# Interleaving early attention with projections and scan inputs, and feeding the late attention with single scan operations and single matmuls

## The chip, the cores and the metric

The kernel runs on one core of one Trainium2 chip. The metric is the device time of that core in microseconds (us), as the median of several executions. A profiled execution also gives a *span*, from its first to its last instruction, which is 1.9 us shorter than the time of the same execution here (180.44 and 178.5 us before). Each execution is marked fast or slow: slow means more than 1.5% above the fastest of the same kernel. Comparisons below use fast executions unless the text says otherwise.

The engines are PE (matmul), PEld (its weight loads, which overlap PE), DVE (vector), ACT (scalar), POOL and SP. SP does nothing here but issue DMAs.

## The reference

Two independent layers read two inputs of 2048 rows by 448 columns. Their outputs stand side by side in the result.

```python
def _A_ref(x, wqkv, wo):                  # local attention, 16 heads of 28
    q, k, v = split_heads(x @ wqkv)
    # row s sees rows s, s-2, ..., s-14 (8 of them, dilation 2)
    attn = softmax(where(mask, q . k[idx] * scale, -1e9))
    return merge_heads(attn . v[idx]) @ wo

def _B_ref(x, ...):                       # complex diagonal state space layer
    Bu = x @ B_bar.T
    for t in range(2048):
        h = Lam_bar * h + Bu[t]           # 448 complex states
    return 2 * real(hs @ Cmat.T) + x * Dskip

return concatenate([a, b], axis=-1)       # 2048 x 896, bfloat16
```

## The kernel before

Even and odd rows are handled apart, so that layer B scans over 1024 pairs of rows and the dilated window of layer A becomes a dense one. Its work comes in these pieces:

- `proj_qk` and `proj_v` (tiles `pq`, `pv`): the projections of layer A.
- `bu(s, pt)` (tile `pb`): scan inputs, for two halves `s` of time and four groups `pt` of states. `scan(s, hf)` is a scan on DVE over two groups.
- `step(n)`: scores (`sp`) of attention block n on PE, the exponential (`P`) on ACT, and the product with the values (`op`) of block n-1. There are 18 blocks.
- Normalization of the attention in three stages, after blocks 7, 13 and 17: the row sums are written to DRAM and read back spread over partitions (`dc`), inverted (`rf`), written to DRAM, read back as a broadcast (`rd`), and multiplied into the attention output (`qT`, the same storage as `oT`).
- `y_tile(n)` (tile `py`): 18 matmuls give 256 output rows of layer B; ACT and DVE each evacuate a half (`yb`). `wo_tile(n)` (tile `pw`): 8 matmuls give 256 output rows of layer A (`ya`).

All of `pq`, `pv`, `pb`, `sp`, `py` and `pw` share three PSUM buffers, called `ps2`. Each engine executes its instructions in the order of the program text once `hold` is set.

```python
def norm_load(k):
    ...                                                # [cut]
    nc.sync.dma_start(s1[:], oT[DH:128:32, :, :, c0:c0 + w_])
    dc = at.tile([128, QB], BF16, tag="dc", name="dc")
    nc.sync.dma_start(dc[0:r_, :], s1[:]...)           # [cut]
    rf = at.tile([128, QB], F32, tag="rf", name="rf")
    V.reciprocal(rf[0:r_], dc[0:r_])
    rb = at.tile([128, QB], BF16, tag="rb", name="rb")
    V.tensor_copy(rb[0:r_], rf[0:r_])
    ...                                                # [cut: a check; s2 <- rb; four broadcasts rd <- s2]

def norm(k):
    V.tensor_tensor(o_, o_, att["rd", k][:]..., ALU.mult)

def scan(s, hf):                                       # 12 to 16 DVE operations in a row
    ...
    V.tensor_tensor(c_, z, sinb, ALU.mult)
    V.tensor_tensor(z, z, cosb, ALU.mult)
    V.tensor_tensor(z[:, 0], z[:, 0], c_[:, 1], ALU.add)
    V.tensor_tensor(z[:, 1], z[:, 1], c_[:, 0], ALU.subtract)
    for ri in range(2):
        for i in range(2):
            V.tensor_tensor_scan(c_[:, ri, i, :], ...)
    ...                                                # [cut: carry if s == 0; then 4 more]

def y_tile(n):
    ps = ps2.tile([128, 2, 512], F32, tag="s", name="py")
    ...                                                # [cut: 11 matmuls into half 0, 7 into half 1]
    ACT.copy(yb[:, 0, :], ps[:, 0, 0:D])
    V.tensor_tensor(yb[:, 1, :], ps[:, 1, 0:D], xD[:, n, :], ALU.add)
    nc.sync.dma_start(out_b[n, :, :, D:2 * D], yb[:])

# after the start: projections of the second half, woven only with small weight products
weave([L(proj_qk, qk, par, 1, gp) for gp, par, qk in QK] + [L(proj_v, b) for b in range(4, NB)], fl)
bz_open()
hold[0] = True

def step(n):
    if n < NA:
        att_s(n)
    if 0 < n <= NA:
        att_pv(n - 1)
        if n in (8, 14, 18):
            norm_load((8, 14, 18).index(n))

for s_ in range(2):
    for pt in range(4):
        bu(s_, pt)
        if pt % 2:
            scan(s_, pt // 2)
        step(4 * s_ + pt)
k0_make(0)
step(8)
k0_make(1)
step(9)
step(10)
for k in range(4):
    if k % 2:
        norm(k // 2)
    y_tile(k)
    step(11 + 2 * k)
    step(12 + 2 * k)
for n in range(3):
    wo_tile(n, "A")
y_tile(4)
for n in range(3, 6):
    wo_tile(n)
y_tile(5)
norm(2)
...                                                    # [cut: y 6, wo 6 and 7, a check, y 7]
```

The loads of `wo` and of `xD` (the odd rows of B's input, for the skip term) are issued from the POOL queue at the start of the program.

## Time and profile before

| | before |
|---|---|
| time, median of 3 | 179.55 us (179.32 to 180.45) |
| span of the profiled execution | 178.5 us |
| PE busy | 141.3 us, 79% |
| DVE busy, ACT busy | 110.3 us, 98.4 us |
| longest idle time of PE | 12.47 us |
| scores of block 8 start | 95.94 us |
| last matmul ends, end of span | 171.3, 178.5 us |

These lines are from the page of the profile of the kernel before: busy shares in tenths in 40 slices of 4.46 us each (9 is 90% or more); PEclk is the granted PE clock in tenths.

```profile
PE   7673896999999989899999891009787969999930
...
DVE  2308999988698108999999999980224040624410
...
PEclk9979699999999999999999998555969999999996
```

From slice 9 to 24 PE is at 8 or 9. In slices 25 to 27 (107 to 120 us) it shows 1, 0, 0, where DVE shows 9, 9, 8, and the clock falls to 5. What happened there is in the timeline of the kernel before. Its columns are the start, the duration, engine and line, operation, output and inputs with shapes, count, and in brackets the idle time before it and what ended it. The full list has ACT and weight loads between these lines.

```profile
105.63 1.22 DVE L135 TENSOR_TENSOR sc<-Z,tab 128x2048 bf16<-128x2048 bf16 x1
...
106.71 0.37 PE L135 MATMUL sp<-mB,mA 32*128 32x456 bf16 x4
...
109.48 4.81 DVE L135 TENSOR_TENSOR_SCAN sc<-rT,ini,Z 128x512 bf16<-128x512 f32 x4
...
116.84 1.29 DVE L135 TENSOR_TENSOR Hs<-Hs,sc 128x1024 bf16<-128x1024 bf16 x2
118.05 0.86 DVE L135 RECIPROCAL rf<-dc 128x114 f32<-128x114 bf16 x1
...
119.40 0.62 DVE L135 TENSOR_TENSOR yb<-py,xD 128x448 bf16<-128x448 f32 x1
120.07 0.57 PE L135 MATMUL sp<-mB,mA 32*128 32x456 bf16 x4 [12.47 <-DVE yb L135]
...
121.46 1.68 PE L135 MATMUL py<-K_178,xTB 128*128 128x448 bf16 x4
```

From 105.63 to 118.05 us DVE works through the last scan, 12.4 us. The reciprocal of the first normalization and its small operations come next, and only at 119.40 us the addition `yb`, which reads the PSUM buffer of y tile 0. PE could issue scores at 106.71 us; for the next ones it needed the buffer of `ps2` that `yb` reads, and waited 12.47 us. The next matmuls of y take 0.42 us each (1.68 us for 4), where those of y tile 0 took 0.21 (1.49 us for 7, not shown): half clock. The Trainium skill ("TensorE: Matmul & The Clock Gate", Part 1) says that an idle window of about 3.4 us lets the clock fall to half, and this agrees.

The list of what PE waited for, in total, times and longest, puts that wait first.

```profile
engine line waited for: us in total, times, longest us
PE sp L135 <- DVE yb L135: 12.5, 1, 12.5
PE sp L135 <- ACT P L135: 2.9, 5, 0.8
```

Busy time of each engine by stretches of the kernel before shows the losses around it (in parentheses the count of instructions):

```profile
core 0: us, PE busy (x) PEld busy (x) DVE busy (x) ACT busy (x) POOL busy (x), PEclk, DMA share, GB/s
...
110.00:120.00 10.00, 0.00 (x0) 0.00 (x0) 9.83 (x13) 0.00 (x0) 0.00 (x0) 0.53 0.00 0
...
130.00:146.00 16.00, 13.05 (x165) 6.56 (x165) 3.90 (x8) 9.76 (x15) 0.00 (x0) 0.89 0.29 78
```

In the gap PE does nothing at all and DVE is busy 9.83 of 10 us. From 130 to 146 us PE is busy 13.05 of 16 us, with pauses for ACT's `P`, which is 1.75 us for each block.

### The profile page before, as it was taken

To read this page: it belongs to the slowest core of one execution; us is meant where nothing else is said; L and a number is where in the kernel's file an instruction comes from. 1 tells how busy PE (TensorE), PEld (TensorE's weight loads), DVE (VectorE), ACT (ScalarE), POOL (GpSimd) and SP (SyncE) were. 2 spreads that over 40 slices of the span, in tenths; PEclk is the share of its full clock that TensorE was granted. 3 is DMA by queue.
4 is the path that set the end of the run, shared out by engine and by line. 5 is a ranking of instruction groups with operands and counts; after the bars stand their busy time and mean duration, and the time that the engine had idled before them with its cause. 6 is when DMAs were issued, how large, how long until landed. Compare 5 with 4: busy or idle time off the path is not lost. (4 is left out here: it accounts for less than half of the span.)

```text
span 178.5 us, 3078 instructions
## 1 busy us (share of the span) xinstructions
PE 141.3 (79%) x1217; PEld 68.6 (38%) x1227; DVE 110.3 (62%) x194; ACT 98.4 (55%) x142; POOL 13.0 (7%) x31
## 2 busy tenths in 40 slices
PE   7673896999999989899999891009787969999930
PEld 2231342444445444444445440004433535555410
DVE  2308999988698108999999999980224040624410
ACT  2006899699886297777777765004645573322210
POOL 8990000000000000000000000000000000000000
PEclk9979699999999999999999998555969999999996
DMA  5999999999900000000000000006411704273320
GB/s 109 202 271 258 285 191 218 184 186 177 210 0 4 0 0 0 4 0 4 0 4 0 13 4 0 0 7 167 99 36 34 190 21 143 76 252 110 105 84 30
DMA packets 34262, 16.40 MB, mean 92 GB/s; under 512 B 27376, under 2 KB 33460, under 8 KB 34244
## 3 DMA queue, kind: packets, MB, share of 16 engines
q1 hardware_dynamic: 33676, 14.55, 35.6%
q0 software_dynamic: 560, 1.61, 3.4%
q8 instruction: 11, 0.18, 0.4%
q14 instruction: 7, 0.06, 0.1%
q10 hardware_dynamic: 8, 0.00, 0.0%
HBM read 5.90 MB, written 3.80 MB: 54 GB/s over the span
## 5 line engine op out<-in xcount | busy, mean ns | idle before, releaser
L135 ACT ACTIVATE P<-sp 128x912 bf16<-128x912 f32 x36 | 31.6, 934 | 12.2 <-PE sp L135 12.1
L137 PE MATMUL pq<-xTA,wqk 128*128 128x512 bf16 x125 | 28.2, 381 | 2.2 <-DVE kT L137 1.7
L135 PE MATMUL pb<-xTB,BT 128*128 128x512 bf16 x105 | 25.1, 379 | 2.6 <-ACT Z L135 2.3
L137 PE MATMUL pv<-wv,xTA 128*128 128x448 bf16 x72 | 17.0, 399 | 4.3 <-ACT vp L137 2.5
L135 PE MATMUL sp<-mB,mA 32*128 32x456 bf16 x72 | 8.0, 371 | 15.6 <-DVE yb L135 12.5
L137 PEld LDWEIGHTS <-wqk 128*128 128x128 bf16 x128 | 12.7, 99 | 17.7 <-issue 3.4
L135 PEld LDWEIGHTS <-BT 128*128 128x128 bf16 x112 | 10.9, 97 | 14.3 <-issue 2.1
L135 ACT CAST yb<-py 128x448 bf16<-128x448 f32 x8 | 4.3, 532 | 22.0 <-PE py L135 22.0
L135 PEld LDWEIGHTS <-Hs 128*128 128x128 bf16 x112 | 11.7, 105 | 12.1 <-issue 3.2
L135 DVE TENSOR_TENSOR qT<-qT,rd 128x3648 bf16<-128x3648 bf16 (+2 forms) x3 | 4.7, 1580 | 15.6 <-DMA rd<-s_1259 8.1
L135 PE MATMUL py<-WL,Hs 128*128 128x448 bf16 x56 | 13.9, 395 | 0.0
L135 ACT CAST Z<-pb 128x1024 bf16<-128x1024 f32 x8 | 8.1, 1012 | 9.4 <-PE pb L135 9.4
L137 PEld LDWEIGHTS <-xTA 128*128 128x128 bf16 x72 | 7.7, 108 | 12.8 <-issue 7.9
L135 PE MATMUL pw<-wo,qT 128*128 128x448 bf16 x64 | 12.6, 353 | 0.0
L135 PE MATMUL py<-Wt,Hs 128*128 128x448 bf16 x56 | 12.2, 359 | 0.0
L135 PEld LDWEIGHTS <-mA 32*128 32x128 bf16 x72 | 2.4, 91 | 21.9 <-issue 21.4
L135 DVE TENSOR_TENSOR sc<-Z,tab 128x2048 bf16<-128x2048 bf16 x4 | 4.9, 1226 | 9.2 <-ACT Z L135 8.9
L135 ACT CAST qT<-op 128x456 bf16<-128x456 f32 x18 | 10.0, 554 | 0.0
L137 DVE CAST kT<-pq 128x1024 bf16<-128x1024 f32 x8 | 9.8, 1222 | 0.2 <-PE pq L137 0.2
L135 DVE TENSOR_TENSOR_SCAN sc<-rT,ini,Z 128x512 bf16<-128x512 f32 x8 | 9.6, 1265 | 0.1
L135 DVE TENSOR_TENSOR yb<-py,xD 128x448 bf16<-128x448 f32 x8 | 5.0, 620 | 7.1 <-ACT yb L135 7.1
L135 DVE RECIPROCAL rf<-dc 128x114 f32<-128x114 bf16 (+2 forms) x3 | 2.6, 859 | 10.9 <-DMA dc<-s_1800 6.4
(142 smaller groups left out, 207.8 us busy)
## 6 DMA issues: line engine op xcount, KB each, us to landing
out_dram<-yb SPq DMA_DIRECT2D x8, 224.0 KB
out_dram<-ya SPq DMA_DIRECT2D x8, 224.0 KB, 2.7
rd<-s_1259 SPq DMA_DIRECT2D x4, 228.0 KB, 5.0
xD<-in_B_x_dram POOLq DMA_DIRECT2D x1, 896.0 KB, 9.2
rd<-s_1599 SPq DMA_DIRECT2D x4, 171.0 KB, 2.7
wraw<-in_A_wqkv_dram SPq DMA_DIRECT2D x3, 224.0 KB
rd<-s_1809 SPq DMA_DIRECT2D x4, 114.0 KB, 2.6
wo<-in_A_wo_dram POOLq DMA_DIRECT2D x4, 98.0 KB, 3.9
```

The source lines that it names most:

```text
L135: r = f(*a, **k)
L137: r = f(*a, **k)
```

## The change

The intent is to take DVE's last scan off the way of PE and to give PE something to do in each pause. It has five parts:

1. *Weave.* `pb` tiles, the second-half projections and attention blocks 0 to 7 are put in one hand-made order, so that scans start early and ACT's exponentials are spread over a longer time. `hold` is set only after the weave; before that the order on an engine need not be that of the text.
2. *Cut scan.* The last scan becomes 12 single DVE operations; two of them follow each attention step.
3. *Nines.* y and wo products become lists of single matmuls, and nine of them are issued after each attention step.
4. *Split reciprocals.* `norm_inv` (the inverse, and the way back through DRAM) is split from `norm_load`, and comes some steps later.
5. *Late loads.* `xD` is loaded near the end of the weave (issued at 84.59 us in the trace) and `wo` after it (99.26 us) rather than at the start, into space that is free by then. The scans also work in place in `Hs`.

The diff holds smaller edits outside these five: `P` gets three buffers instead of two, some loads and transposes at the start come in another order, the scheduler may choose the engine that evacuates the second-half projections, and DVE instead of ACT copies wo tiles 0 to 2.

```diff
@@ norm_load @@
         nc.sync.dma_start(dc[0:r_, :], s1[:]...)          # [shortened]
-        rf = at.tile([128, QB], F32, tag="rf", name="rf")
+        att["dc", k] = dc
+
+    def norm_inv(k):
+        dc = att["dc", k]
+        rf = zz["at"].tile([128, QB], F32, tag="rf", name="rf")
         V.reciprocal(rf[0:r_], dc[0:r_])
@@ y_tile, in the same way wo_tile @@
-    def y_tile(n):
+    def y_parts(n):
+        t = {}
+        def mm(i, lhs, rhs, start, stop):
+            if not t:
+                t["ps"] = ps2.tile([128, 2, 512], F32, tag="s", name="py")
+            PE.matmul(t["ps"][:, i, 0:D], lhs, rhs, start=start, stop=stop)
+            if i and stop:
+                ...                                        # [cut: evacuation and store]
+        return [L(mm, 0, xTB[:, kt, xs], K0[:, kt, :], kt == 0, False) for kt in range(4)] + ...
@@ scan: the same operations as a list, scan_parts(s, hf) [cut] @@
@@ late loads @@
-    for j in range(4):
-        POOL.dma_start(wo[32 * j:32 * j + DH, :, :], wo_r[j])
-    POOL.dma_start(xD[:, 0:n_, :], B_x[0]...[1])
+    def late_open():
+        pj_ctx.close()
+        ...                                                # [cut: wo loaded here]
+    def xd_load():
+        xD = zz["xD"] = st.tile([128, n_ + 1, D], BF16, tag="NB", name="xD")
+        POOL.dma_start(xD[:, 0:n_, :], B_x[0]...[1])
@@ main part @@
-    weave([L(proj_qk, ...)] + [L(proj_v, b) for b in range(4, NB)], fl)
-    bz_open()
-    hold[0] = True
-    for s_ in range(2):
-        for pt in range(4):
-            bu(s_, pt)
-            if pt % 2:
-                scan(s_, pt // 2)
-            step(4 * s_ + pt)
-    ...
+    for x in "pbwpbwpsbwpspwbsplblpsblplskbpkpsbpkspsp":
+        {"p": PJ, "b": BU, "s": ST, "w": WM, "l": WLM, "k": KM}[x].pop(0)()
+    for s_, hf in ((0, 0), (0, 1), (1, 0)):
+        scan(s_, hf)
+    late_open()
+    hold[0] = True
+    fill = []
+    dq = scan_parts(1, 1)
+
+    def spend(k, d=0):
+        while k > 0 and fill:
+            fill.pop(0)()
+            k -= 1
+        for _ in range(d):
+            if dq:
+                dq.pop(0)()
+
+    skip_make()
+    for n in range(4):
+        fill += y_parts(n)
+    for n in range(8, NA + 1):
+        step(n)
+        if n == 11:
+            norm_inv(0)
+        if n == 14:
+            norm(0)
+            for k in range(3):
+                fill += wo_parts(k, "D")
+            fill += y_parts(4)
+        if n == 17:
+            norm_inv(1)
+        spend(9, 2)
+    spend(10)
+    norm(1)
+    for k in range(3, 6):
+        fill += wo_parts(k, "D")
+    spend(18)
+    norm_inv(2)
+    spend(1000)
+    for n in (5, 6):
+        fill += y_parts(n)
+    spend(1000)
     norm(2)
     ...                                                    # [cut: wo 6 and 7, check, y 7]
```

## The prediction

> **What bounds the kernel now.** The span is 178.5 us; the busy table gives PE 141.3 (79%), DVE 110.3, ACT 98.4. The table by stretches of 10 us shows three parts. From 28 to 107 us PE is dense (9 to 10 of each 10 us). From 107.5 to 120.07 PE does nothing while DVE is full: the timeline has the whole last scan, then a reciprocal, and only then the `yb` of y tile 0. The list of waits has "PE sp <- DVE yb 12.5 us": the next scores need the PSUM buffer that this `yb` reads. After it matmuls issue every 0.37 us for a while, against 0.19 later. From 120 to 146 us PE also pauses 0.5 to 0.8 us at each pair of attention blocks, waiting for ACT's P (1.76 us a block). There the chain of waits runs through PE; from the last matmul (171.3) to the end are 7.2 us.
>
> From 102.5 to 171.3 us (68.8) PE had 8 y tiles (18 matmuls at 0.187 = 3.36 us each), 8 wo tiles (1.49) and 8 attention steps (about 0.82): 45.4 us of work. So about 23 us are lost.
>
> **What the change does.** It adds and removes almost no work; it moves it. (1) The `pb` tiles, the second-half projections and attention blocks 0 to 7 are woven: first scan at about 49 us, against 67.4. (2) The last scan is cut into 12 pieces, two per attention step, so `yb` waits for about 2.5 us of DVE work instead of 9 or more. (3) y and wo products are issued nine matmuls (1.7 us) after each attention step, just what covers ACT's 1.76. The reciprocals are split from their loads; the xD and wo loads (1.3 MB) move from the crowded start to later.
>
> **Arithmetic, by hand with the trace's durations.** In the weave PE has about 54 us left after the first `pb` (done about 43.5), ACT about 48, with three PSUM buffers. Stepping through it I get the scores of block 8 at about 100.5 us, no better than before (95.9): weaving dense work gains nothing by itself. After that PE has 46.6 us. Added waits:
> - ACT at 2.6 us per step against PE's 2.5: 1.4 us.
> - Second normalization: inverse to broadcast took 8.3 us (136.2 to 144.7), plus 1.6 for the product; PE has about 6 us of filler: 4 us idle.
> - Third: 2 us idle.
> - Cold clock after those: 1.5 us.
>
> PE ends near 156.5; the end of 7.2 us makes a span of 164, and with 1 us between span and time, 165.
>
> **On the critical path:** gained are 12.5 us of idle, some 4 of half clock, 3 to 4 of ACT pauses and a few others; lost are 5 us of later attention and 6 to 8 of normalization waits: about 14.5 net.
>
> The Trainium skill ("TensorE: Matmul & The Clock Gate", Part 1) says an idle window of about 3.4 us drops the clock to half; this trace agrees after the 12.5 us idle (0.37 against 0.19 us). So whether the normalization stalls stay below that matters.
>
> **Predicted time: 165 us, 8 in 10 between 159 and 172.** Faster by over 2%: 0.94; within 2%: 0.04; slower: 0.02.
>
> **Right if the profile shows:** no PE idle over 5 us after 40 us; PE busy above 85%; first scan before 52 us; scores of block 8 at 97 to 104; DVE `yb` no longer the first wait; new waits of DVE `qT` for the DMA `rd`, and PE `pw` waiting for DVE `qT` 2 to 5 us.
>
> **Wrong if:** ACT is overloaded in the weave (block 8 after 106); the xD load, which reuses the NB buffer, lands late and blocks DVE; or the normalization waits exceed 5 us each and let the clock drop.

## The result, and the profile after

| | before | after |
|---|---|---|
| time, median | 179.68 us (179.32 to 180.45, 4 runs) | 163.41 us (163.43, 163.23, 163.38 fast; 167.03 slow) |
| ratio of the fast runs, 95% interval | 1 | 0.9086, 0.9048 to 0.9124 |
| span of the profiled execution, granted clock | 178.5 us, 0.924 | 161.6 us, 0.995 |
| PE busy | 141.3 us, 79% | 135.7 us, 84% |
| first scan starts | 67.44 us | 44.85 us |
| scores of block 8 start | 95.94 us | 97.24 us |
| last matmul ends | 171.3 us | 155.0 us |
| longest idle time of PE after 40 us | 12.47 us | 2.34 us |

A ratio is the mean time of one kernel's fast runs over that of the other's of the same rounds, so it is not quite the ratio of the medians quoted. The output is correct.

The same rows of the page, of the changed kernel (a slice is 4.04 us here):

```profile
PE   7575699989989979999999999898897977994930
...
DVE  3009999995589999999999640399855536815310
...
PEclk9999999999999999999999999999999999999997
```

The gap in PE's row is gone and the clock stays at 9 to the last slice but one. PE has nearly the same instructions; 5.6 us of its busy time are gone where matmuls took longer before: the groups of instructions show 399 and then 352 ns for one `pv` matmul, and 395 and then 353 ns for one of `py` with `WL`.

Where the time came from can be read by stage. From the scores of block 8 to PE's last matmul went 171.3 - 95.94 = 75.4 us before, and 155.0 - 97.24 = 57.8 us after: 17.6 us less. To the scores of block 8 the changed kernel takes 1.3 us *more*, and the end after the last matmul shrank by 0.6 us. Together that is the 16.9 us between the spans. (One of the two `K0` products stood after block 8 before, from 97.07 to 100.12 us, and stands in the weave now. So some 3 us of the 17.6 are work that moved to the stage in front, which in turn began 2.2 us earlier: its first `pq` starts at 18.67 instead of 20.86 us.)

The timeline of the changed kernel around y tile 0, which answers to the one shown of before:

```profile
101.55 1.49 PE L135 MATMUL py<-Wt,Hs 128*128 128x448 bf16 x7
...
103.68 0.62 DVE L135 TENSOR_TENSOR yb<-py,xD 128x448 bf16<-128x448 f32 x1 [8.73 <-ACT yb L135]
...
104.36 0.92 PE L135 MATMUL py<-K_172,xTB 128*128 128x448 bf16 x4 [0.50 <-DVE yb L135]
...
105.54 1.28 DVE L135 TENSOR_TENSOR_SCAN sc<-rT,ini,Hs 128x512 bf16<-128x512 f32 x1
```

Now `yb` of y tile 0 starts 0.64 us after its last matmul ends at 103.04, with pieces of the scan behind it, and PE waits 0.50 us instead of 12.47. The new waits stand in the list of what PE waited for in the changed kernel:

```profile
PE pw L135 <- DVE qT L135: 4.4, 2, 2.3
...
PE py L135 <- DVE yb L135: 1.4, 3, 0.5
```

The first of them are the second and the third normalization. This is the second, in the timeline of the changed kernel; `s_1790` is the DRAM buffer in the middle of the way back:

```profile
125.60 0.31 SPq L395 DMA_DIRECT2D s_1790<-rb  x1
...
127.15 1.70 SPq L398 DMA_DIRECT2D rd<-s_1790  x4
...
130.79 1.49 PE L135 MATMUL py<-Wt,Hs 128*128 128x448 bf16 x7
...
132.66 1.58 DVE L135 TENSOR_TENSOR qT<-qT,rd 128x2736 bf16<-128x2736 bf16 x1 [2.66 <-DMA rd<-s_1790]
...
134.30 3.96 PE L135 MATMUL pw<-wo,qT 128*128 128x448 bf16 x20 [2.03 <-DVE qT L135]
```

The inverse is sent to DRAM at 125.60 us, the four broadcasts are issued from 127.15 us, and the last one lets the multiplication on DVE start at 132.66 us. PE's fill work, here the last 7 matmuls of y tile 4, is used up at 132.28 us, so it waits 2.03 us. The third normalization costs 2.34 us at 148.17 us in the same way.

Busy time by stretches of the changed kernel, with the columns of before; from 121 to 155 us is where PE still idles:

```profile
98.00:121.00 23.00, 21.22 (x372) 11.00 (x364) 14.77 (x18) 19.60 (x29) 3.34 (x5) 1.00 0.38 96
121.00:137.00 16.00, 12.80 (x125) 6.33 (x118) 8.31 (x12) 5.46 (x9) 0.00 (x0) 1.00 0.40 120
137.00:155.00 18.00, 15.63 (x82) 7.61 (x80) 7.43 (x16) 1.97 (x3) 0.00 (x0) 1.00 0.37 118
```

### The profile page after: what moved, and what is told of

The parts are those of the page before. It is cut to its first block, busy times and chain, and to the rows that moved or that the text cites. A ratio compares the mean times of both kernels' runs of the same rounds, so it can differ in the third digit from the quotient of the medians.

```text
span 161.6 us, 3078 instructions
## 1 busy us (share of the span) xinstructions
PE 135.7 (84%) x1218; PEld 65.5 (41%) x1227; DVE 109.2 (68%) x195; ACT 96.9 (60%) x141; POOL 12.8 (8%) x31
## 4 chain that ended last, share of the span: by engine, by line
PE 43%; DVE 22%; ACT 15%; DMA 8%; SPq 5%; issue 3%; DVEq 0%; ACTq 0%
PE py L135 12%; PE pb L137 11%; PE pw L135 6%; PE pq L137 4%; DVE sc L137 4%; PE pk L137 4%; ACT P L135 3%; PE pv L137 3%; DVE Hs L137 3%; DMA rd<-s_1790 3%; SPq L200 2%; ACT P L137 2%; DMA wraw<-in_A_wqkv_dram 2%; DMA BT<-NB__94 2%; DVE NB__94 L137 2%
## 5 line engine op out<-in xcount | busy, mean ns | idle before, releaser
L135 ACT ACTIVATE P<-sp 128x912 bf16<-128x912 f32 x20 | 17.6, 939 | 5.4 <-PE sp L135 5.4
L137 PEld LDWEIGHTS <-wqk 128*128 128x128 bf16 x128 | 12.5, 97 | 18.1 <-issue 3.6
L137 PE MATMUL pv<-wv,xTA 128*128 128x448 bf16 x72 | 14.9, 352 | 5.3 <-POOL K_172 L496 1.9
L135 DVE TENSOR_TENSOR yb<-py,xD 128x448 bf16<-128x448 f32 x8 | 5.0, 624 | 16.9 <-ACT yb L135 16.8
L135 PEld LDWEIGHTS <-Hs 128*128 128x128 bf16 x112 | 10.7, 98 | 9.9
L135 DVE CAST ya<-pw 128x896 bf16<-128x896 f32 x7 | 7.5, 1087 | 7.8 <-PE pw L135 7.8
L135 PE MATMUL py<-WL,Hs 128*128 128x448 bf16 x56 | 12.6, 353 | 0.0
L137 ACT CAST Hs<-pb 128x1024 bf16<-128x1024 f32 x8 | 8.0, 1004 | 7.0 <-PE pb L137 7.0
L135 PEld LDWEIGHTS <-qT 128*128 128x128 bf16 x64 | 5.9, 98 | 11.0 <-DVE qT L135 5.2
L137 DVE TENSOR_TENSOR_SCAN sc<-rT,Hs 128x512 bf16<-128x512 f32 x8 | 9.1, 1204 | 0.1
L135 PE MATMUL py<-K_172,xTB 128*128 128x448 bf16 x32 | 7.4, 352 | 1.8 <-DVE yb L135 1.4
L137 DVE TENSOR_TENSOR Hs<-Hs,sc 128x1024 bf16<-128x1024 bf16 x12 | 7.8, 687 | 0.2
L137 ACT COPY wqk<-wraw 128x896 bf16<-128x896 bf16 (+1 forms) x2 | 1.9, 936 | 9.0 <-DMA wraw<-in_A_wqkv_dram 8.9
```

The costliest lines, as they stand in the source:

```text
L135: r = f(*a, **k)
L137: r = f(*a, **k)
```

## The experiments

All twelve kernels gave correct results. They ran in four batches, each on one chip, with runs of the kernel before beside them (median 180.4 to 180.8 us in each). Only one batch holds the unaltered changed kernel (ref_after), so most variants are compared with it across chips. In the first batch single runs of the kernel before spread from 178.2 to 182.7 us, and its verdicts were recorded as unclear (none for e_inv_at_load, which has one fast run), although the intervals lie well below 0.98; differences of a microsecond between batches should not be read.

The first theory was: the idle time comes from the last scan's position on DVE in front of `yb`, so that cutting it is what counts. The rival was: the early start of the scans (the weave) is what counts.

### a_split_only: the kernel before with only the last scan cut

```diff
+    dq = scan_parts(1, 1)        # the 12 operations of scan(1, 1) as a list
     for s_ in range(2):
         for pt in range(4):
             bu(s_, pt)
-            if pt % 2:
+            if pt % 2 and (s_, pt) != (1, 3):
                 scan(s_, pt // 2)
     ...
         y_tile(k)
+        pieces(2)                # issues the next 2 of dq
         step(11 + 2 * k)
+        pieces(2)
         step(12 + 2 * k)
```

> The kernel before with one thing changed: the last scan is cut into its 12 pieces, two after each y tile or attention step from y tile 0 on; no weave, no nines, loads as before. Theory 1 (the gain comes from taking the undivided last scan out of the way of yb, by whatever means): the 12.5 us idle of PE goes, and most of the half clock after it; but the product of the first normalization now waits on DVE for its broadcast ahead of yb of y tile 1, which may cost PE up to 5 us. 164 to 170 us, PE idle before a scores matmul under 2 us. Rival 1 (the weave, that is the earlier start of the scans, makes the gain, and cutting alone only spreads the same DVE work): 174 us or more.

Measured: 167.55 us in the median (fast runs 166.55 to 167.56), ratio 0.930 (0.921 to 0.938). The profiled execution was slow; in it the wait of 12.5 us is gone:

```profile
108.52 0.62 DVE L135 TENSOR_TENSOR yb<-py,xD 128x448 bf16<-128x448 f32 x1 [0.53 <-ACT yb L135]
...
109.20 0.67 PE L135 MATMUL sp<-mB,mA 32*128 32x456 bf16 x4 [0.45 <-DVE yb L135]
```

The scores that had waited 12.47 us now wait 0.45 us, and the longest wait of scores for ACT's `P` is 0.8 us. The wait of up to 5 us that was feared for y tile 1 did not come (the longest wait of `py` for a `yb` is 0.8 us). One part of the five, by itself, gives three quarters of the gain (1 - 0.930 against 1 - 0.909). The rival, that it needs the weave, falls.

### c_whole_scan: the changed kernel with the last scan whole again

```diff
     skip_make()
+    while dq:
+        dq.pop(0)()
```

> The changed kernel with the last scan issued whole, after the product for xD and before the first yb. Theory 1 in its strict form (the cut is needed): yb 0 waits about 12 us again and the time is 170 us or more. Theory 2 (weave or cut is enough, either one): the scan then runs from about 92.5 to 104.8 us, yb of y tile 0 is wanted at 103.1, so PE loses only 1 to 2 us: 164 to 166 us.

Measured: 166.11 us (165.03 to 167.37), ratio 0.923 (0.914 to 0.932). With scans started early, `yb` of y tile 0 came at 105.31 instead of 103.68 us, and PE's longest wait for a `yb` was 1.9 us. So cutting is worth only 2 to 3 us *in the presence of the weave*. The strict form of the theory, "only the cut counts", falls as well: the early scans, with the rest of the change around them, remove most of the same wait without the cut. (The weave alone, in the kernel before, was not run.)

### g_no_weave: the changed kernel with the old order of the early work

```diff
-    for x in "pbwpbwpsbwpspwbsplblpsblplskbpkpsbpkspsp":
+    for x in "pwpwpwpwplplplplpppppHbsbcsbsbcsbsbcsbsbskkk":   # c: a whole scan, H: hold[0] = True
```

> The changed kernel with the weave undone: all second-half projections and weight preparation first, then pb with attention blocks 0 to 7 and the scans in order, then the products for y; from block 8 on as changed (pieces, nines, split normalization, late loads). If the weave matters because it starts the scans earlier: the first scan starts about 60 us, xD and the pieces about 10 us later than PE needs them, PE waits about 5 us for yb of y tile 0: 167 to 172 us. If the pieces make it unnecessary: 163 to 165 us.

Measured: 168.95 us (fast 167.41, 168.01, 169.90), ratio 0.933 (0.925 to 0.941), against 164.15 us of the unaltered changed kernel in the same batch. The timeline of this kernel shows what the weave had been protecting:

```profile
101.55 2.02 DVE L135 TENSOR_TENSOR xD<-xD 128x3584 bf16<-128x3584 bf16 x1
...
105.88 0.62 DVE L135 TENSOR_TENSOR yb<-py,xD 128x448 bf16<-128x448 f32 x1
...
106.55 1.65 PE L135 MATMUL py<-K,xTB 128*128 128x448 bf16 x4 [5.02 <-DVE yb L135]
```

The third scan ends later, so the skip product (`xD`, 2.02 us) starts at 101.55 us instead of 90.54. It and the first pieces of the last scan (from 103.48 us) stand in front of `yb` of y tile 0, which comes at 105.88 us; PE waits 5.02 us for it, and the next four matmuls run at half clock (1.65 us). Undoing the weave costs about 4.3 us (the difference of the fast means, 168.4 and 164.1 us). In its own stage, though, the weave costs time: without it the scores of block 8 start at 95.09 us instead of 97.24, after the same start (first `pq` at 18.75 and 18.67 us) and the same work. The edit also sets `hold` at its old place, so the freedom to reorder is undone with the weave.

### d_no_nines: whole y tiles after every second step

```diff
-        spend(9, 2)
-    spend(10)
+        spend(18 if n % 2 else 0, 2)
+    spend(19)
```

> The changed kernel with the 18 matmuls of a y tile issued together after every second attention step, instead of nine after each. If the nines cover ACT's 1.76 us per block: about 1.2 us more of pauses per pair of blocks, five pairs, less about 0.5 us per pair saved elsewhere: 3 to 5 us slower, 166.5 to 168.5 us. If they do nothing: 163.4 us.

Measured: 165.06 us (fast 162.79 to 165.13), ratio 0.920 (0.912 to 0.928). In the traces two steps and 18 matmuls take 6.29 us (103.69 to 109.98) instead of 5.82 (100.33 to 106.15), so the nines do cover some of ACT's time. But the profiled execution, 162.79 us, was as short as any of the changed kernel: in it PE waited only once for the normalization, 2.3 us, instead of twice, 4.4 us. Being later at the second normalization, it found it done. What the nines gain is handed back at the next wait, at least in part: 0 to 2 us remain (fast means 164.4 against 163.4 and 164.1 us), and this test does not say which. Neither expectation, 166.5 to 168.5 or 163.4 us, was met.

### e_inv_at_load: each reciprocal directly after its load, as before

```diff
         att["dc", k] = dc
+        norm_inv(k)
...
-        if n == 11:
-            norm_inv(0)
...                               # [cut: the other two calls go too]
```

> The changed kernel with each reciprocal issued straight after the loads of its sums, as in the kernel before. If the separation matters: DVE stands before the reciprocal until dc lands (3 to 5 us each), holding back yb and the scan: 2 to 6 us slower for stages 1 and 2, partly paid back because the broadcasts are there sooner (the two waits of pw for qT, 4.4 us in sum, shrink). Net 164 to 168 us. If it is idle motion: 163.4 us within 0.5.

Measured: 179.54 us in the median; one fast run of 175.07 us and three slow ones of 179.5 to 179.9. No theory expected that much: the fast run is 11.7 us above the changed kernel's fast mean of 163.35 (another batch, on another chip). Its timeline, from a slow execution, shows where the loss begins:

```profile
90.78 2.03 DVE L135 TENSOR_TENSOR xD<-xD 128x3584 bf16<-128x3584 bf16 x1 [1.48 <-PE pb L137]
...
103.64 0.35 SPq L383 DMA_DIRECT2D dc<-s  x1
...
105.48 0.87 DVE L135 RECIPROCAL rf<-dc 128x114 f32<-128x114 bf16 x1 [12.68 <-DMA dc<-s]
...
109.91 0.56 PE L135 MATMUL sp<-mB,mA 32*128 32x456 bf16 x2 [2.87 <-DVE yb L135]
```

The reciprocal stands behind the skip product in DVE's order, but its data `dc` has still to come through DRAM: the load is issued at 103.64 us. DVE waits 12.68 us for it, from 92.8 to 105.48 us, and everything behind it, all pieces of the scan and `yb`, waits too. The Trainium skill ("TensorE: Matmul & The Clock Gate", Part 1, "Architectural detail: the array is 16× 32×32, not 1× 128×128") calls the queues of ACT and DVE strict FIFO; this wait agrees.

The 12.68 us are idle time of DVE, not of PE. PE waits 2.87 us for `yb`, works at half clock for a while, and starts y tile 2 at 116.12 us, where the changed kernel starts it at 110.15. So the first wait makes about 6 us of lag. At the start of y tile 4 the lag is 12.6 us (141.28 against 128.71). What adds to it is a wait of 3.31 us for the normalized `qT` and half clock after it (nine matmuls of `pw` take 3.54 us instead of 1.88). Over the whole trace PE waits 9.6 us for `qT` in three waits, against 4.4 us in two, and is busy 148.0 us with the work that took 135.7. This trace is a slow one, so how the 11.7 us of the fast run divide among the waits and the clock stays open.

In the kernel before, this position did no harm at the first reciprocal: it came behind a scan of 12.4 us, and its data was there (no wait is shown at 118.05 us; the second and third waited 4.5 and 6.4 us, and the list of PE's waits shows none behind them). In a_split_only, too, the first follows the scan before it without a wait; only the third waits, 8.4 us. So the cut alone does not need the split reciprocals. With the scans started early they are needed, here with the cut and in the next run without it, and the prediction gave them no value.

### j_whole_inv_load: both of the last two

```diff
     skip_make()
+    while dq:
+        dq.pop(0)()
...
+        norm_inv(k)              # at the end of norm_load, and not where it was
```

> The changed kernel with the last scan whole and each reciprocal straight after its load: the weave without cutting and without splitting the normalization. If the loss with the reciprocal at its load (175 to 180 us) came from the first reciprocal waiting for dc in front of the scan pieces and yb, the whole scan now fills that wait and the first stage costs under 2 us; what remains is the second reciprocal's 4 us wait and its sequel: 167 to 171 us. If splitting the normalization matters in itself: 175 us or more.

Measured: 173.65 us (173.22 to 174.41), ratio 0.963 (0.957 to 0.968), between the two expectations. The whole scan gave the first reciprocal time, as in the kernel before: it waited 0.20 us. But the second waited 5.55 us and the third 4.68 us, and PE waited 10.4 us in 3 for normalized `qT`. The head-of-queue wait comes back wherever no long DVE work hides it.

### ref_after: the changed kernel again, unaltered

> The changed kernel itself, unaltered, so that the variants have it on the same chip: 163.4 us, 161 to 166.

Measured: 164.15 us (164.87, 163.44, 164.93, 163.30), ratio 0.909 (0.903 to 0.915). This batch's chip repeats the gain. Its profiled execution, 164.87 us, is useful beside the first one, 163.43 us. After the second normalization's wait (2.29 us in this trace, 2.03 us in the other) its 24 matmuls of `pw` read

```profile
134.28 6.40 PE L135 MATMUL pw<-wo,qT 128*128 128x448 bf16 x24 [2.29 <-DVE qT L135]
```

6.40 us, where the other execution shows 4.71 us in the same grouping. A pause of nearly the same length led to half clock here and not there.

### f_tail: the end in another order

The two waits of 2.03 and 2.34 us were the largest left, so the wo tiles that need the second normalization were put behind y tile 5 and the third inverse, and wo tiles 6 and 7 last.

```diff
-    spend(10)
-    norm(1)
-    for k in range(3, 6):
-        fill += wo_parts(k, "D")
-    spend(18)
-    norm_inv(2)
     spend(1000)
-    for n in (5, 6):
-        fill += y_parts(n)
+    norm(1)
+    fill += y_parts(5)
     spend(1000)
-    norm(2)
+    norm_inv(2)
     ...                          # [cut: the check]
-    fill += wo_parts(6) + wo_parts(7)
+    for k in range(3, 6):
+        fill += wo_parts(k, "D")
+    fill += y_parts(6)
     ...                          # [cut: the check's end, y 7]
+    norm(2)
+    fill += wo_parts(6) + wo_parts(7)
```

> The changed kernel with its end in another order: y tile 4 is finished and y tile 5 is made before wo tiles 3 to 5, y tiles 6 and 7 are made before wo tiles 6 and 7, and the check of the sums moves ahead of y tile 7. The two waits of pw for the product qT (2.0 and 2.3 us) should go; no work is added. 4 us faster than the changed kernel: 159 us. If the waits only move to another place (the third broadcast then lands later than the work lasts), less than 2 us faster.

Measured: 165.41 us (165.02 to 166.22), ratio 0.917 (0.911 to 0.922): 1.4 us slower than the changed kernel of the same batch, a miss. From the timeline of this kernel:

```profile
138.02 0.56 SPq L383 DMA_DIRECT2D dc<-s  x1
...
140.16 0.86 DVE L135 RECIPROCAL rf<-dc 64x114 f32<-64x114 bf16 x1 [2.81 <-DMA dc<-s]
...
143.24 1.65 PE L135 MATMUL py<-K,xTB 128*128 128x448 bf16 x4 [2.57 <-DVE ya L135]
```

The load of `dc` stood in the SP queue behind a store that itself waited for `yb` of y tile 5, and was issued at 138.02 us. The third reciprocal waited 2.81 us for it on DVE, in front of the `ya` copies, and PE waited 2.57 us for a `ya`; four matmuls then took 1.65 us, half clock. The wait had been moved, not removed, in the same manner as in e_inv_at_load.

### h_tail_no_nines: f_tail without nines

```diff
-        spend(9, 2)
+        spend(18 if n % 2 else 0, 2)
```

> The kernel with the reordered end, but y tiles issued whole after every second attention step. In the changed kernel the nines took 5.8 us per pair of steps against 6.3 without them, and the time was the same. Theory: the nines gain 2 to 2.5 us in the attention stage and the wait for the second normalization takes it back; where that wait is filled they should show: 1.5 to 2.5 us slower than with the nines. Rival: the nines are worth nothing anywhere: within 0.5 us.

Measured: 168.04 us (fast 166.45, 167.48, 168.60; 169.03 in the slow, profiled one), ratio 0.928 (0.920 to 0.935), 2.0 us above f_tail in the fast means. The size fits the expectation, but the end of f_tail was faulty, so this supports the reading of the nines and does not settle it.

### f2_tail: the same order, mended

The loads and stores of the third normalization go to the POOL queue, where no output stands in front of them. wo tiles 3 to 5 are copied by ACT, and the multiplication of the third stage is issued before y tile 7.

```diff
-        nc.sync.dma_start(dc[0:r_, :], ...)                     # likewise s2 <- rb and rd <- s2
+        (POOL if k == 2 else nc.sync).dma_start(dc[0:r_, :], ...)
     norm(1)
+    norm_inv(2)
     fill += y_parts(5)
     spend(1000)
-    norm_inv(2)
     ...
-        fill += wo_parts(k, "D")
+        fill += wo_parts(k, "A")
     ...
+    norm(2)
     fill += y_parts(7)
     spend(1000)
-    norm(2)
     fill += wo_parts(6) + wo_parts(7)
```

> The reordered end, mended where its first version failed: there the load of the third sums stood in SP's queue behind an output waiting for yb of y tile 5, the third reciprocal then stood on DVE in front of the copies of wo tiles 3 to 5, and the third product stood behind yb of y tile 7. Now the third stage's four transfers go by POOL's queue, ACT copies wo tiles 3 to 5, and the third product is issued before y tile 7. If the in-order queues were the cause: both waits of pw for qT under 0.5 us, no wait of py for ya, 3 to 5 us faster than the changed kernel: 159 to 161 us. If the round trip itself is too long for the work at hand: 162 us or more.

Measured: **158.18 us** (158.01 to 158.89, 6 runs), ratio 0.877 (0.873 to 0.881), span 156.2 us, PE busy 87%. It beats both kernels. No line of PE waiting for `qT` is left; in the stage after the weave these are the two longest entries in the list of what PE waited for:

```profile
PE py L135 <- DVE yb L135: 1.4, 3, 0.5
...
PE sp L135 <- DVE ya L135: 0.7, 1, 0.7
```

So the two normalization waits, with what followed them, were worth 5 to 6 us (fast means 158.3 against 163.4 and 164.1 us, on other chips). The third round trip is still long (inverse issued to DRAM at 137.31, product at 145.31 us), but y tiles cover it. The edit changes the order, the queue and the engine of the copies at once; what each gives was not separated.

### i_early_copies: is it the late loads that let the start run earlier?

In the changed kernel the first `pq` starts at 18.67 us instead of 20.86, and this was not in the prediction's sum. To test it the two loads were repeated early, into space that is overwritten before anything reads it.

```diff
+    Hs = bz.tile([128, 8, NP + 2], BF16, tag="Hs")
+    for j in range(4):
+        POOL.dma_start(Hs[32 * j:32 * j + DH, 4:8, 500:500 + D], wo_r[j])
...
+    POOL.dma_start(Hs[:, :, 2:2 + D], B_x[0]...[1])
+    POOL.dma_start(Hs[:, 0, 500:500 + D], B_Dskip...)
```

> The changed kernel, which in addition loads xD, Dskip and wo at their old early place into memory that is overwritten later and that nothing reads (the late loads stay). If moving those 1.3 MB off the start is what makes the first projections start earlier: pq starts near 20.9 us again instead of 18.7, and the time rises by 1.5 to 2.5 us, to about 166. If the start gained from something else: pq at 18.7 and under 0.5 us.

Measured: 170.72 us (169.02 to 171.12), ratio 0.942 (0.936 to 0.948). `pq` started at 26.24 us, much later than expected. The reason is in the order of issues: in the kernel before a memset of `wo` stood ahead of these loads on POOL; without it those of `wo` were issued 2.5 us earlier (5.04 instead of 7.53 us), so that all came ahead of the loads of `wraw`, and that of `xD` 1.7 us earlier. The direction was right, the size was not that of the change.

### k_early_as_before: the same with POOL's old order

```diff
+    POOL.memset(Hs[:, 4:8, 500:500 + D], 0.0)      # then as in i_early_copies
```

> As the early copies, but with POOL's queue in exactly the order of the kernel before: first a memset as long as that of wo (1.68 us), then one Cx load, wo, the other Cx loads, xD, Dskip. The first early copies stood 2.5 us too early, ahead of wraw, and cost more than the kernel before can have paid. If the crowding of the start is worth what the first projections show between the two kernels (pq at 20.9 against 18.7 us): pq at 20.5 to 21.5, and 165.5 to 167 us. If the loads cost 6 us wherever they stand: pq above 24, about 170 us.

Measured: 171.43 us (fast 169.57, 171.21, 171.65), ratio 0.959 (0.947 to 0.970). Three timelines belong together. This is the start of the kernel before (a transpose load of `xTA`, the first `pq`, the issue of the `BT` transposes):

```profile
15.52 5.33 SPq L201 DMA_TRANSPOSE xTA<-in_A_x_dram  x1
...
20.86 0.59 PE L137 MATMUL pq<-xTA,wqk 128*128 128x512 bf16 x1 [0.15 <-DVE vp L137]
```

This is the start of the changed kernel, with its first `pb`:

```profile
14.24 2.15 SPq L200 DMA_TRANSPOSE xTA<-in_A_x_dram  x1
...
18.67 7.07 PE L137 MATMUL pq<-xTA,wqk 128*128 128x512 bf16 x31 [1.43 <-DVE vp L137]
...
32.52 10.61 SPq L509 DMA_TRANSPOSE BT<-NB__94  x8
...
35.82 3.19 PE L137 MATMUL pb<-xTB,BT 128*128 128x512 bf16 x14 [0.80 <-DMA BT<-NB__94]
```

And this is k_early_as_before:

```profile
15.51 5.87 SPq L200 DMA_TRANSPOSE xTA<-in_A_x_dram  x1
...
21.30 0.64 PE L137 MATMUL pq<-xTA,wqk 128*128 128x512 bf16 x1
...
38.47 10.61 SPq L515 DMA_TRANSPOSE BT<-NB__94  x8
...
41.60 3.20 PE L137 MATMUL pb<-xTB,BT 128*128 128x512 bf16 x14 [3.74 <-DMA BT<-NB__94]
```

`pq` starts at 21.30 us, as expected. But the time is over 4 us above the 165.5 to 167 us that went with it. The first `pb` needs `BT`, whose transposes are issued by SP behind all the others: 38.47 us instead of 32.52. One `xTA` transpose takes 5.87 us of issue where the changed kernel shows 2.15 and the kernel before 5.33. PE waits 3.74 us for `BT` and starts `pb` 5.8 us later than in the changed kernel. The Trainium skill ("Trainium Kernel Development and Optimization", Key Constraints) says that DMAs from the SP, ACT and POOL queues run on the same 16 DMA engines and interleave; that loads on POOL lengthen transposes on SP agrees with it.

In the kernel before, the crowding did not delay `pb`: its first `pb` ran at 58.8 us, and the last `BT` transposes were issued by 47.6 us. The weave moves `pb` to the start, and so makes the loads critical for it; the late loads then make room. But the crowding was not free before either. g_no_weave, which has the old order of the early work with late loads, starts the scores of block 8 at 95.09 us with both `K0` products done; the kernel before starts them at 95.94 with one of them (3.05 us) still to come. How much of these 3.9 us is due to the loads, and how much to the smaller edits at the start, is open: the late loads alone were not run in the kernel before.

## Why the prediction was right, and which terms were off

**The bound and the cause were right.** The prediction put the loss on one wait of 12.5 us behind the last scan. The trace after has no such wait, and a_split_only, with the cut scan alone, removes it and gives three quarters of the gain. The three signs named for it came true: no idle time of PE over 5 us after 40 us (longest 2.34), first scan before 52 us (44.85), scores of block 8 between 97 and 104 us (97.24). PE busy above 85% was narrowly missed (84%). Of the waits named as new, PE's `pw` for DVE's `qT` came (2.03 and 2.34 us). DVE's `qT` for the broadcast `rd` came too (2.66 us), but it was not new: in the kernel before DVE waited 8.13 and 7.49 us for `rd`, with no wait of PE behind it.

**"Weaving gains nothing by itself" was half right.** In its own stage the weave even costs 2.2 us (block 8 at 97.24 us, and at 95.09 in g_no_weave). But g_no_weave is 4.3 us slower as a whole, because scans done early leave DVE free for `yb` in the later stage. The prediction's own figure for the first scan (49 against 67.4 us) pointed there, and it drew no value from it.

**The sum, term by term.** The predicted span was 164 us, measured 161.6.

| term | predicted | measured |
|---|---|---|
| first `pb` done (the next matmul starts) | 43.5 us | 38.86 us |
| weave, from there to the scores of block 8 | 57 us | 58.4 us |
| PE work after that | 46.6 us | about 50.4 us |
| pauses in steps | 1.4 us (ACT) | about 3.0 us (all but normalization) |
| second and third normalization | 4 + 2 us | 2.03 + 2.34 us |
| cold clock | 1.5 us | none in this trace |
| end after the last matmul | 7.2 us | 6.6 us |
| from span to time | 1 us | 1.8 us |

The measured work and pauses come from the stretches shown: from 98 to 155 us PE is busy 21.22 + 12.80 + 15.63 = 49.65 us and idle 7.35 us, of which 4.37 us are the two normalizations; 0.76 us from 97.24 to 98 are added to the work. (The prediction's terms from block 8 on add up to 56.0 us with rounding; measured were 57.8.)

The largest mis-sized term is the first. The prediction listed the late loads and gave them no value; i_early_copies and k_early_as_before show that the start depends on them: `pb` starts at 35.82 us in the changed kernel, and at 41.60 us where the loads are repeated early, and the time is about 7 us longer (fast means 170.8 and 163.4 to 164.1 us). The two terms of work and pauses were too small by 5.4 us, which almost cancels the first. That the sum came within 2.4 us of the span is thus in part luck. The clock term was not wrong in kind: in ref_after the same wait did lead to half clock.

**What the prediction left out** is how the parts hold each other up. Undoing one part alone costs about 2 to 3 us for the cut, 4.3 for the weave, 0 to 2 for the nines, about 7 for the late loads, and about 12 for the split reciprocals (one fast run). That is 25 us or more, out of a total gain of 16.3. These are not shares of the gain; they are the harm that appears when one part has lost the other's protection. The prediction's "split reciprocals" had no number in it at all, and that was the costliest part to take back.

**The end left room.** The prediction saw the normalization waits of 4 and 2 us as given. f2_tail shows that they could be covered by another order and another queue, for another 5 to 6 us.

## What to carry to other kernels

When a long chain on one engine stands in front of a short evacuation that frees a PSUM buffer, cut the chain or start it earlier; here either removed most of the wait, so do not add their gains. Anything that waits for a DMA must not enter an in-order queue before its data is due: place the load early, and the operation that uses it late, and look at what stands in front of the load in its own queue as well. When work is moved to the start of a program, look again at every load there that used to have time.

## What the Trainium skill lacked or had wrong

- "TensorE: Matmul & The Clock Gate", Part 1, ties the drop to half clock to an idle window of about 3.4 us. The 12.47 us wait agrees (0.42 instead of 0.21 us a matmul). But shorter pauses did it too, and not always: 2.29 us in ref_after (granted clock 0.72 from 134 to 136 us and 0.50 from 136 to 138) and 2.57 us in f_tail did, while 2.03 and 2.34 us in the changed kernel's first trace left it at 1.00. In the kernel before, a wait of 0.72 us at 130.4 us, after several others, was followed by 0.50 from 132 to 134 us. The page's section "A second HAM failure mode: psum-queue depth-cycling" says that frequent small idle times can make the clock oscillate, but gives no length for them; the runs here show none either, only that 3.4 us in one piece are not needed.
- None of the pages looked up gives the cost of turning a small tile round through DRAM into a broadcast. Here, from the issue of the inverse's write to the product: 7.06 us in the changed kernel (125.60 to 132.66 us) and 8.0 us in f2_tail's third stage (137.31 to 145.31). "DMA: Bandwidth & Descriptors", "Anatomy of one DMA — SWDGE (gpsimd) path", has the fixed cost of one transfer issued by POOL; this way has two steps, a write and then four broadcasts, issued by SP in the first case and by POOL in the second.
- "Trainium Kernel Development and Optimization", Key Constraints, says that queues interleave on the same engines, but not how much the position in a queue decides: the same extra loads, issued 1.7 to 2.5 us earlier or later on POOL, gave a first `pq` at 26.24 or at 21.30 us.
- The strict FIFO of ACT and DVE stands in an architectural detail of the page on TensorE. Nothing there says what follows for a short operation that waits for a DMA at the head of such a queue; in e_inv_at_load DVE stood idle 12.68 us in one such wait, and PE lagged by about 6 us after it.
